# Half-merged weight words and the row norm's root in PSUM, and a second bank for the MLP's second products

## The chip, the cores and the metric

The kernel runs on one core of a Trainium2 chip. The metric is the device time of one execution in microseconds. The chip's engines appear under the names of the profile: PE (TensorE, matrix products), PEld (its weight loads), DVE (VectorE), ACT (ScalarE), POOL (GpSimd) and SP, which issues DMA transfers. SBUF is the on-chip memory, PSUM the banks that PE writes its products into; DVE and ACT read and write both.

## The reference

Three layers follow each other; their inputs are fp32, the first one's shape is (2 samples, 8 heads, 768 tokens, 64).

```python
# 1 attention within buckets
q_bits = (einsum('bhsd,dk->bhsk', q, proj) > 0);  k_bits likewise       # 6 bits
mask = q_bucket[:, :, :, None] == k_bucket[:, :, None, :]
scores = where(mask, q @ k.T / 8, -1e9)
x = softmax(scores) @ v                      # -> (2, 768, 512)
# 2 Fourier mixing and an MLP
u = x + real(fft(fft(x, axis=1), axis=2))
un = (u - mean(u)) / sqrt(var(u) + 1e-6)
x = u + maximum(un @ w_ch1, 0) @ w_ch2       # 512 -> 2048 -> 512
# 3 gated MLP
h = gelu(x @ w_in);  u, v = halves of h      # 512 -> 1024
v_s = w_sg @ (layernorm(v) * g_ln) + b_sg    # over the 768 tokens
out = x + (u * v_s) @ w_out
```

The weights arrive as 64-bit floats, and the kernel makes 32-bit ones of them on the chip.

## The kernel before

Each product that needs fp32 accuracy is made of three f16 products: both factors are split into a high part and a residue (`hl`, `h`, the two halves of a weight region), and `HH` lists the three pairs. So a matrix that is used must be loaded, brought to 32 bits, scaled by a power of two and split.

*Weights.* `weight` (L197 to L239) does this for every matrix. It loads a matrix in pieces into a buffer `wide` (L215). For each piece three DVE steps shift and combine the two 32-bit halves of every word: L219 and L220 work on the high half and leave a half-merged word `t`, L221 adds the low half. Result and half-merged word lie in the same place, the matrix's region. The second MLP matrix, `w2`, has 8 regions of 1024 columns in two pieces each, so 16 pieces of 512; there are two `wide` buffers for it. `w_in` (16 pieces of 256), `w_out` (8) and `w_sg` come later, also with two buffers. After the last piece of a matrix the sum of its squares goes through one PE instruction (`pb`, L136), which gives the scale.

*Sample 0 and sample 1.* Attention works through the heads of sample 0 and then of sample 1. Per group of 128 queries there are a reduction on DVE (`nm`, L397), the exponential on ACT (L399), and a split of it on POOL (`eh`, L251; 128x768 elements). The FFT of a sample ends in tiles of 128 rows `xu` (L590, L591), whose mean and variance are collected (L599, L600). `norm` (L607) then makes 1/sqrt of the variance (`rsqrt`, L108: a first guess by integer steps and three rounds of L115 to L117), scales the rows by a power of two (`un`, L631), splits them (ACT L632, POOL L633) and has them transposed by a DMA into `unT`. For sample 0 all six tiles share one root (6 elements a row), for sample 1 each pair of tiles has its own.

*The MLP.* `ch` (L639) takes 256 rows at a time, a chunk; there are three chunks for a sample. A chunk has 16 groups c1 of 12 matmuls (L657, into a bank of `self.pp`), each followed by a relu on ACT (L663) and its residue on DVE (`h`, L664); sample 1 has 17 buffers for `h`. Then come the second products c2, for each half of the chunk 48 matmuls (L674) into one bank, the only one of the pool `pc`; L678 multiplies it by the row's factor, adds the tile of `xu` and so empties the bank.

*Order.* Three streams are merged by weights: `second` (the rest of attention, then sample 1's FFT), `main0` (sample 0's FFT and MLP) and `prep2` (`w2`). Later the MLP of sample 1 is merged with `side`, which brings the weights of the third layer. A scheduler that follows modelled times then fixes the order of the instructions of each engine from data and buffers; on the chip each engine takes its own queue strictly in that order. `pc` is opened after sample 0's attention; c1 uses the two banks of `pp` and `pp2` in turn until attention is over, and six banks after that. Attention's output has a bank of its own in the pool `pa` (tag `pav`), free once attention is done.

Of the kernel before, what the change touches and what calls it, by code (L numbers as in the profile page):

```python
# [9 lines left out]
F32 = mybir.dt.float32  # L10
FR = mybir.dt.float32r
F16 = mybir.dt.float16
I32 = mybir.dt.int32
AF = mybir.ActivationFunctionType
ALU = mybir.AluOpType
# [5 lines left out]
P = 128  # L21
# [25 lines left out]
LN1 = (True, False)  # L47
# [54 lines left out]
class Kern:  # L102
    def __init__(self, tc, I, out):
        self.tc, self.nc, self.I, self.out = tc, tc.nc, I, out
        self.W = {}


    def rsqrt(self, pool, x, n):  # L108
        nc = self.nc
        y = pool.tile([P, n], F32, tag="rs_y", name="rs_y", bufs=2)  # L110
        t = pool.tile([P, n], F32, tag="rs_t", name="rs_t", bufs=2)
        nc.vector.tensor_scalar(out=y.bitcast(I32), in0=x.bitcast(I32), scalar1=1, scalar2=None, op0=ALU.logical_shift_right)
        nc.vector.tensor_scalar(out=y.bitcast(I32), in0=y.bitcast(I32), scalar1=-1.0, scalar2=float(0x5F3759DF), op0=ALU.mult, op1=ALU.add)
        for _ in range(3):
            nc.vector.tensor_tensor(out=t, in0=y, in1=y, op=ALU.mult)  # L115
            nc.vector.scalar_tensor_tensor(out=t, in0=t, scalar=-0.5, in1=x, op0=ALU.mult, op1=ALU.mult)
            nc.vector.scalar_tensor_tensor(out=y, in0=t, scalar=1.5, in1=y, op0=ALU.add, op1=ALU.mult)  # L117
        return y

# [77 lines left out]
    def weight(self, pool, nm, src, regions, spare, c, q):  # L197

        nc = self.nc
        wide = src.dtype == mybir.dt.int64  # L200
        src = src.bitcast(I32) if wide else src
        sub = WSUB.get(nm, 4)
        m = c // sub
        n = len(regions)
        s, i = self.sc[nm]
        acc = pool.tile([P, 8], F32, tag="wacc", name="wacc", bufs=1)
        tot = pool.tile([P, 1], F32, tag="wm", name="wm", bufs=1)
        for j in range(n):
            if not wide:
                q.dma_start(out=regions[j], in_=src[:, j * c:(j + 1) * c])  # L210
                yield 0.3
            for hf in range(sub if wide else 0):
                o = j * c + hf * m
                x = self.stp.tile([P, 2 * m], I32, tag="wide", name="wide", bufs=self.wb)
                q.dma_start(out=x, in_=src[:, 2 * o:2 * (o + m)])  # L215
                xv = x.rearrange("p (n w) -> p n w", w=2)
                lo, hi = xv[:, :, 0], xv[:, :, 1]
                t = regions[j][:, hf * m:(hf + 1) * m].bitcast(I32)
                nc.vector.tensor_scalar(out=t, in0=hi, scalar1=3, scalar2=0x3FFFFFFF, op0=ALU.logical_shift_left, op1=ALU.bitwise_and)  # L219
                nc.vector.scalar_tensor_tensor(out=t, in0=hi, scalar=-0x40000000, in1=t, op0=ALU.bitwise_and, op1=ALU.bitwise_or)  # L220
                nc.vector.scalar_tensor_tensor(out=t, in0=lo, scalar=29, in1=t, op0=ALU.logical_shift_right, op1=ALU.bitwise_or)  # L221
                yield 0.0029 * m
            nc.scalar.activation(spare[:, 0:c], regions[j], AF.Square, accum_out=acc[:, j:j + 1])
            yield 0.0005 * c
        nc.vector.tensor_reduce(tot, acc[:, 0:n], axis=AX.X, op=ALU.add)
        self.norm_pow2(tot, 2.0 ** 54, s, i, self.pc if nm == "w2" else None)
        yield 1.0
        views = []
        dst = spare
        for j in range(n):  # L230
            d = dst[:, 0:c].bitcast(F16).rearrange("p (t c) -> p t c", t=2)
            nc.scalar.activation(d[:, 0, :], regions[j], AF.Copy, scale=i)
            yield 0.0005 * c
            nc.vector.scalar_tensor_tensor(out=d[:, 1, :], in0=regions[j], scalar=i, in1=d[:, 0, :], op0=ALU.mult, op1=ALU.subtract)
            views.append(d)
            dst = regions[j]
            yield 0.0005 * c
        self.W[nm] = views
        self.spare = dst  # L239
# [367 lines left out]
    def norm(self, fp, up, b, unT, mv, ts):  # L607
        nc, XU = self.nc, self.XU[b]
        t0, w = ts[0], 2 * len(ts)
        x, e, i, s = (fp.tile([P, w], F32, tag=f"ln{j}", name=f"ln{j}", bufs=1 if LN1[b] else 2) for j in range(4))  # L610
        nc.vector.tensor_scalar(out=x.rearrange("p (a c) -> p a c", c=2), in0=mv[:, t0:ts[-1] + 1, :, 1], scalar1=EPS, scalar2=None, op0=ALU.add)
        nc.vector.tensor_scalar(
            out=e.bitcast(I32), in0=x.bitcast(I32), scalar1=24, scalar2=23, op0=ALU.logical_shift_right, op1=ALU.logical_shift_left
# [1 line left out]
        nc.vector.tensor_scalar(  # L615
            out=i.bitcast(I32), in0=e.bitcast(I32), scalar1=-1.0, scalar2=float(190 << 23), op0=ALU.mult, op1=ALU.add
        )
        rs = self.rsqrt(fp, x, w)
        nc.vector.reciprocal(s, i)
        nc.vector.tensor_tensor(out=self.tok[b][:, 2 * t0:2 * t0 + w], in0=rs, in1=s, op=ALU.mult)  # L620
        yield 0.9
# [17 lines left out]
    def ch(self, hp, b, unT, step, tags=None):  # L639
# [27 lines left out]
        def c2(n, j, f):  # L667
            w2 = self.W["w2"]
            if f == 0:
                self.c2t = self.pc.tile([P, 512], F32, tag="c2", name="c2")  # L670
            ps = self.c2t
            wv = w2[f // 2].rearrange("p t (k c) -> p t k c", k=2)[:, :, f % 2, :]
            for m, (a, w) in enumerate(HH):
# [141 lines left out]
    def build(self):  # L815
# [3 lines left out]
        with ExitStack() as ctx:  # L819
# [47 lines left out]

            def second():
                yield from att
                c_att.close()  # L870
                c_s2.close()
                pp3 = c_ps.enter_context(tc.tile_pool(name="pp3", bufs=4, space=PSUM))
# [113 lines left out]
```

## Time and profile before

| | |
|---|---|
| time, median of 3 runs (lowest to highest) | 722.25 us (721.98 to 722.77) |
| the profiled execution: its time, its span | 724.48 us, 722.7 us |
| mean granted clock of TensorE, share of full speed | 0.943 |
| busy time of PE, DVE, ACT, POOL | 645.0, 503.9, 329.8, 273.7 us |
| matmuls: c1 (L657) / c2 (L674) | 1152 in 136.8 us / 576 in 131.8 us |
| three steps of the unpacking of `w2`, 16 pieces | L219 9.0, L220 16.8, L221 17.7 us |

The span is the time from the first to the last instruction of the profiled execution. An engine's busy time says how long it worked, not whether anything waited for it; stretches of some 20 us, the chain of waits that ended last, and single instructions of the timeline show that. An instruction's duration in the timeline includes time in which it has begun and is held up inside, so the same instruction can have two durations. Which part belongs to which time: sample 0's attention ends at about 182 us, the unpacking of `w2` goes from there to 283 us, the rest of attention and sample 1's FFT go on to about 430 us, the MLP of sample 1 ends at 578 us, and the third layer takes the rest.

### The profile page before, as it was taken

The numbers are of one execution on the slowest core, as the hardware profiler recorded it, in microseconds if no ns is written. First come the engines' busy times: TensorE is split into PE (matmuls) and PEld (weight loads), VectorE is DVE, ScalarE is ACT, GpSimd is POOL, SyncE is SP. The second block draws the span as 40 slices with busy tenths as digits, with TensorE's granted clock in tenths as the row PEclk, the third lists the DMA queues.
The fourth block names the chain that finished last, engine by engine and source line by source line (L and its number), as shares of the span: only waits on it lengthen the run. The fifth ranks groups of instructions, "written<-read, shape, count | busy, mean of one in ns | idle before, by whom it ended". The sixth has DMA issues, their size and how long they took to land.

```text
span 722.7 us, 12521 instructions
## 1 busy us (share of the span) xinstructions
PE 645.0 (89%) x4828; PEld 421.8 (58%) x4828; DVE 503.9 (70%) x1095; ACT 329.8 (46%) x517; POOL 273.7 (38%) x232
## 2 busy tenths in 40 slices
PE   3788987976876578999999999979999999999997
PEld 0666677764563357658865766736668444444443
DVE  6999598658999997745435694867562266777663
ACT  5766687764664556745632421423642044222110
POOL 2568588879486465536455041000000012111000
PEclk8899999996886879999999999989999999999999
DMA  8969787999798989737563036552000012011334
GB/s 310 312 182 213 140 175 143 204 202 259 158 235 169 212 193 211 140 67 152 101 128 108 2 60 221 125 148 91 1 1 1 1 35 53 15 29 18 86 88 117
DMA packets 182428, 92.24 MB, mean 128 GB/s; under 512 B 166240, under 2 KB 167008, under 8 KB 181344
## 3 DMA queue, kind: packets, MB, share of 16 engines
q1 hardware_dynamic: 181792, 91.30, 55.0%
q8 instruction: 38, 0.62, 0.4%
q10 hardware_dynamic: 576, 0.14, 0.1%
q14 instruction: 22, 0.18, 0.1%
HBM read 39.50 MB, written 3.15 MB: 59 GB/s over the span
## 4 chain that ended last, share of the span: by engine, by line
PE 56%; DVE 21%; DMA 12%; POOL 4%; issue 3%; ACT 2%; SPq 0%; DVEq 0%; POOLq 0%; ACTq 0%
PE c L674 13%; PE c L657 12%; PE gi L739 9%; PE sg L762 6%; PE s L387 4%; PE go L779 4%; DMA wide<-w_in 3%; DMA et<-eh 3%; DMA wide<-w 3%; DVE nm L397 2%; DVE w L221 2%; DVE w L220 2%; POOL eh L251 2%; DVE k L258 1%; PE y L542 1%
## 5 line engine op out<-in xcount | busy, mean ns | idle before, releaser
L251 POOL TENSOR_TENSOR eh<-e,eh 128x768 f16<-128x768 f32 x80 | 143.4, 1796 | 53.7 <-ACT eh L244 51.0
L657 PE MATMUL c<-unT,w 128*128 128x256 f16 x1152 | 136.8, 277 | 4.2 <-DVE h L664 4.2
L674 PE MATMUL c<-w,h 128*128 128x512 f16 x576 | 131.8, 384 | 5.3 <-DVE xu L678 5.3
L657 PEld LDWEIGHTS <-w 128*128 128x128 f16 x1152 | 113.0, 99 | 22.6 <-issue 5.3
L387 PE MATMUL s<-k,q 128*128 128x384 f32 x384 | 108.1, 413 | 17.8 <-ACT k L282 7.4
L399 ACT ACTIVATE e<-s,nm 128x768 f32<-128x768 f32 x96 | 85.3, 896 | 55.3 <-DVE nm L397 44.7
L397 DVE TENSOR_REDUCE nm<-s 128x1 f32<-128x768 f32 x96 | 90.3, 948 | 22.6 <-PE s L387 21.5
L674 PEld LDWEIGHTS <-h 128*128 128x128 f16 x576 | 56.2, 99 | 69.6 <-issue 9.2
L755 POOL TENSOR_TENSOR vh<-gv,vh 128x512 f16<-128x512 f32 x12 | 13.9, 1156 | 214.0 <-ACT vh L754 214.0
L387 PEld LDWEIGHTS s<-k,q 128*128 128x128 f32 x384 | 72.0, 211 | 30.1 <-ACT k L282 8.3
L455 PE MATMUL pav<-V,et 128*128 128x65 f16 x480 | 56.4, 199 | 19.2 <-DMA et<-eh 13.8
L664 DVE SCALAR_TENSOR_TENSOR h<-c,h 128x256 f16<-128x256 f32 x96 | 39.8, 419 | 36.3 <-ACT h L663 35.8
L246 POOL TENSOR_SCALAR eh<-e 128x768 f16<-128x768 f32 x48 | 47.9, 999 | 36.8 <-ACT e L399 30.7
L455 PEld LDWEIGHTS <-et 128*128 128x128 f16 x480 | 46.0, 102 | 26.1 <-DMA et<-eh 17.7
L456 PE MATMUL pav<-V,et 128*128 128x64 f16 x480 | 56.2, 197 | 0.0
L457 PE MATMUL pav<-V,et 128*128 128x65 f16 x480 | 56.2, 199 | 0.0
L456 PEld LDWEIGHTS <-et 128*128 128x128 f16 x480 | 46.5, 101 | 7.7 <-issue 6.9
L739 PE MATMUL gi<-in,xT 128*128 128x512 f16 x216 | 50.5, 379 | 0.0
L663 ACT ACTIVATE h<-c 128x256 f16<-128x256 f32 x96 | 34.6, 377 | 34.6 <-PE c L657 34.2
L739 PEld LDWEIGHTS <-xT 128*128 128x128 f16 x288 | 28.2, 98 | 35.0 <-issue 1.1
L457 PEld LDWEIGHTS <-et 128*128 128x128 f16 x480 | 46.5, 101 | 1.5 <-issue 0.8
L762 PE MATMUL sg<-vh,sg 128*128 128x512 f16 x180 | 40.8, 379 | 0.0
(198 smaller groups left out, 1009.9 us busy)
## 6 DMA issues: line engine op xcount, KB each, us to landing
wide<-w SPq DMA_DIRECT2D x8, 1024.0 KB, 8.9
wide<-w SPq DMA_DIRECT2D x16, 512.0 KB, 4.3
x<-qk SPq DMA_DIRECT2D x16, 384.0 KB, 4.5
k<-q SPq DMA_DIRECT2D x26, 192.0 KB, 4.1
wide<-w_in SPq DMA_DIRECT2D x16, 256.0 KB, 3.5
vst<-v SPq DMA_DIRECT2D x8, 396.0 KB, 5.3
y<-ot SPq DMA_DIRECT2D x12, 256.0 KB, 2.3
q<-q SPq DMA_DIRECT2D x13, 192.0 KB, 3.9
```

The lines of the kernel that those rows point to most:

```text
L246: self.nc.gpsimd.tensor_scalar(out=out, in0=src, scalar1=scale, scalar2=1.0, op0=ALU.mult, op1=ALU.mult)
L251: (self.nc.vector if eng == "D" else self.nc.gpsimd).tensor_tensor(out=out, in0=a, in1=b, op=ALU.subtract)
L387: nc.tensor.matmul(s[:, hf, 0:HS], q[:, qs], k[:, hf * HS:(hf + 1) * HS], start=n == 0, stop=n == len(pairs) - 1)
L397: nc.vector.tensor_reduce(nm, x["s"], axis=AX.XY, op=ALU.max, negate=True)
L399: nc.scalar.activation(e.rearrange("p (a c) -> p a c", a=2), x["s"], AF.Exp, bias=nm)
L455: nc.tensor.matmul(pv[:, qt, 0:65], et[:, kb, :], V[:, hl, kb, 64:129], start=kb == 0, stop=False)
L456: nc.tensor.matmul(pv[:, qt, 0:64], et[:, kb, :], V[:, hl, kb, 0:64], start=False, stop=False)
L457: nc.tensor.matmul(pv[:, qt, 0:65], et[:, NT + kb, :], V[:, hl, kb, 64:129], start=False, stop=kb == NT - 1)
L657: nc.tensor.matmul(ps[:, 0:step], w[:, a, fo], uT[:, 4 * u + kc, o * P:o * P + step], start=m == 0, stop=m == 11)
L674: nc.tensor.matmul(ps, hs[n, f][:, a, j * P:(j + 1) * P], wv[:, w, :], start=f + m == 0, stop=f == NF - 1 and m == 2)
L739: nc.tensor.matmul(ps, xT[:, 4 * a + kc, :], w_in[kc][:, w, half * DM:(half + 1) * DM], start=n == 0, stop=n == 11)
L762: nc.tensor.matmul(ps, w_sg[kt][:, w, t * P:(t + 1) * P], vh[b][:, kt, a, :], start=n == 0, stop=n == 17)
```

## The change

The half-merged word of `w2` gets a tile `wt` of its own in the PSUM bank of `pc`: L219 and L220 write there, L221 reads it and writes the region. In `norm` two of the root's tensors, the variance x and the temporary t, lie in one tile `lnp` in a bank of `self.pp`; in every round the root first multiplies x*y and then that by -0.5*y, in place of y*y and -0.5*x, also for the third layer, whose t stays in SBUF. Once attention is over, odd c2 tiles take the bank of `pa` and even ones that of `pc`.

```diff
--- before.py
+++ after.py
@@ -103,17 +103,18 @@
     def __init__(self, tc, I, out):
         self.tc, self.nc, self.I, self.out = tc, tc.nc, I, out
         self.W = {}
-
-
-    def rsqrt(self, pool, x, n):
+        self.c2n, self.att_over = 0, False
+
+
+    def rsqrt(self, pool, x, n, t=None):
         nc = self.nc
         y = pool.tile([P, n], F32, tag="rs_y", name="rs_y", bufs=2)
-        t = pool.tile([P, n], F32, tag="rs_t", name="rs_t", bufs=2)
+        t = pool.tile([P, n], F32, tag="rs_t", name="rs_t", bufs=2) if t is None else t
         nc.vector.tensor_scalar(out=y.bitcast(I32), in0=x.bitcast(I32), scalar1=1, scalar2=None, op0=ALU.logical_shift_right)
         nc.vector.tensor_scalar(out=y.bitcast(I32), in0=y.bitcast(I32), scalar1=-1.0, scalar2=float(0x5F3759DF), op0=ALU.mult, op1=ALU.add)
         for _ in range(3):
-            nc.vector.tensor_tensor(out=t, in0=y, in1=y, op=ALU.mult)
-            nc.vector.scalar_tensor_tensor(out=t, in0=t, scalar=-0.5, in1=x, op0=ALU.mult, op1=ALU.mult)
+            nc.vector.tensor_tensor(out=t, in0=x, in1=y, op=ALU.mult)
+            nc.vector.scalar_tensor_tensor(out=t, in0=t, scalar=-0.5, in1=y, op0=ALU.mult, op1=ALU.mult)
             nc.vector.scalar_tensor_tensor(out=y, in0=t, scalar=1.5, in1=y, op0=ALU.add, op1=ALU.mult)
         return y
 
@@ -215,10 +216,11 @@
                 q.dma_start(out=x, in_=src[:, 2 * o:2 * (o + m)])
                 xv = x.rearrange("p (n w) -> p n w", w=2)
                 lo, hi = xv[:, :, 0], xv[:, :, 1]
-                t = regions[j][:, hf * m:(hf + 1) * m].bitcast(I32)
+                to = regions[j][:, hf * m:(hf + 1) * m].bitcast(I32)
+                t = self.pc.tile([P, 512], F32, tag="c2", name="wt")[:, 0:m].bitcast(I32) if nm == "w2" else to
                 nc.vector.tensor_scalar(out=t, in0=hi, scalar1=3, scalar2=0x3FFFFFFF, op0=ALU.logical_shift_left, op1=ALU.bitwise_and)
                 nc.vector.scalar_tensor_tensor(out=t, in0=hi, scalar=-0x40000000, in1=t, op0=ALU.bitwise_and, op1=ALU.bitwise_or)
-                nc.vector.scalar_tensor_tensor(out=t, in0=lo, scalar=29, in1=t, op0=ALU.logical_shift_right, op1=ALU.bitwise_or)
+                nc.vector.scalar_tensor_tensor(out=to, in0=lo, scalar=29, in1=t, op0=ALU.logical_shift_right, op1=ALU.bitwise_or)
                 yield 0.0029 * m
             nc.scalar.activation(spare[:, 0:c], regions[j], AF.Square, accum_out=acc[:, j:j + 1])
             yield 0.0005 * c
@@ -607,7 +609,9 @@
     def norm(self, fp, up, b, unT, mv, ts):
         nc, XU = self.nc, self.XU[b]
         t0, w = ts[0], 2 * len(ts)
-        x, e, i, s = (fp.tile([P, w], F32, tag=f"ln{j}", name=f"ln{j}", bufs=1 if LN1[b] else 2) for j in range(4))
+        e, i, s = (fp.tile([P, w], F32, tag=f"ln{j}", name=f"ln{j}", bufs=1 if LN1[b] else 2) for j in range(3))
+        ps = self.pp.tile([P, 512], F32, tag="p", name="lnp")
+        x, r = (ps[:, 8 * j:8 * j + w] for j in range(2))
         nc.vector.tensor_scalar(out=x.rearrange("p (a c) -> p a c", c=2), in0=mv[:, t0:ts[-1] + 1, :, 1], scalar1=EPS, scalar2=None, op0=ALU.add)
         nc.vector.tensor_scalar(
             out=e.bitcast(I32), in0=x.bitcast(I32), scalar1=24, scalar2=23, op0=ALU.logical_shift_right, op1=ALU.logical_shift_left
@@ -615,7 +619,7 @@
         nc.vector.tensor_scalar(
             out=i.bitcast(I32), in0=e.bitcast(I32), scalar1=-1.0, scalar2=float(190 << 23), op0=ALU.mult, op1=ALU.add
         )
-        rs = self.rsqrt(fp, x, w)
+        rs = self.rsqrt(fp, x, w, r)
         nc.vector.reciprocal(s, i)
         nc.vector.tensor_tensor(out=self.tok[b][:, 2 * t0:2 * t0 + w], in0=rs, in1=s, op=ALU.mult)
         yield 0.9
@@ -667,7 +671,9 @@
         def c2(n, j, f):
             w2 = self.W["w2"]
             if f == 0:
-                self.c2t = self.pc.tile([P, 512], F32, tag="c2", name="c2")
+                self.c2n += 1
+                other = self.att_over and self.c2n % 2
+                self.c2t = (self.pa if other else self.pc).tile([P, 512], F32, tag="pav" if other else "c2", name="c2")
             ps = self.c2t
             wv = w2[f // 2].rearrange("p t (k c) -> p t k c", k=2)[:, :, f % 2, :]
             for m, (a, w) in enumerate(HH):
@@ -867,6 +873,7 @@
 
             def second():
                 yield from att
+                self.att_over = True
                 c_att.close()
                 c_s2.close()
                 pp3 = c_ps.enter_context(tc.tile_pool(name="pp3", bufs=4, space=PSUM))
```

In the changed kernel line numbers of what follows are one to six higher: L219 is L221 there, L631 L635, L664 L668, L674 L680, L678 L684, and L115 to L117 are L116 to L118.

First place, DVE at the root of sample 0's norm, in the stretch in which `w2` is unpacked (`w_3_2155` and `w_2_2154` are regions of `w2`, `ln_2856` is x, `bst` and `mv` mean and variance, `k`, `vmx`, `sv` and `iv` belong to attention). Before:

```order
L600 BN_AGGR mv<-bst 128x2
L220 SCALAR_TENSOR_TENSOR w_3_2155<-wide,w_3_2155 128x512
L148 RECIPROCAL iv_106<-sv_105 128x1
L611 TENSOR_SCALAR ln_2856<-mv 128x6
L221 SCALAR_TENSOR_TENSOR w_3_2155<-wide,w_3_2155 128x512
L612 TENSOR_SCALAR ln_2857<-ln_2856 128x6
L112 TENSOR_SCALAR rs_y<-ln_2856 128x6
L615 TENSOR_SCALAR ln_2858<-ln_2857 128x6
```

Changed:

```order
L223 SCALAR_TENSOR_TENSOR w_2_2154<-wide,wt 128x512
L615 TENSOR_SCALAR lnp<-mv 128x6
L149 RECIPROCAL iv_106<-sv_105 128x1
L221 TENSOR_SCALAR wt<-wide 128x512
L616 TENSOR_SCALAR ln_2866<-lnp 128x6
L113 TENSOR_SCALAR rs_y<-lnp 128x6
L222 SCALAR_TENSOR_TENSOR wt<-wide,wt 128x512
L619 TENSOR_SCALAR ln_2867<-ln_2866 128x6
```

The half-merged word now carries the name `wt`, and only L223 names the region; x is `lnp`. The root's first steps stand between the steps of a piece before and after, but about one piece of `w2` earlier.

Second place, PE in the MLP of sample 1, at the end of the first chunk's first second product (c_5910 before, c_5922 in the changed kernel; h_5906 and h_5918 are its last h). Before:

```order
L674 LDWEIGHTS h_5906
L674 MATMUL c_5910<-w_6_2158,h_5906 128x512
L657 LDWEIGHTS w_0_148
L657 MATMUL c_6053<-unT,w_0_148 128x256
L657 LDWEIGHTS w_0_148
L657 MATMUL c_6053<-unT,w_0_148 128x256
```

Changed:

```order
L680 LDWEIGHTS h_5918
L680 MATMUL c_5922<-w_6_2158,h_5918 128x512
L680 LDWEIGHTS h_5614
L680 MATMUL c_5998<-w_8_156,h_5614 128x512
L680 LDWEIGHTS h_5614
L680 MATMUL c_5998<-w_8_156,h_5614 128x512
```

Before, 28 matmuls of the next chunk's c1 follow (c_6053 and on), in the changed kernel the 48 of the chunk's other second product, c_5998, and only then c1.

Third place, DVE at the same time (`in_5614` is the last region of `w_in`, `out_6149` and `out_6150` are the regions of `w_out`, h_6066 and h_6078 the first h of the next chunk). Before:

```order
L219 TENSOR_SCALAR in_5614<-wide 128x256
L220 SCALAR_TENSOR_TENSOR in_5614<-wide,in_5614 128x256
L678 SCALAR_TENSOR_TENSOR xu_82<-c_5910,tok_133,xu_82 128x512
L221 SCALAR_TENSOR_TENSOR in_5614<-wide,in_5614 128x256
L219 TENSOR_SCALAR in_5614<-wide 128x256
L703 TENSOR_REDUCE rmx<-xu_82 128x1
L220 SCALAR_TENSOR_TENSOR in_5614<-wide,in_5614 128x256
L664 SCALAR_TENSOR_TENSOR h_6066<-c_6053,h_6066 128x256
```

Changed:

```order
L223 SCALAR_TENSOR_TENSOR out_6149<-wide,out_6149 128x256
L728 TENSOR_TENSOR hs<-x_s,s_in 128x1 x2
L222 SCALAR_TENSOR_TENSOR out_6150<-wide,out_6150 128x256
L684 SCALAR_TENSOR_TENSOR xu_82<-c_5998,tok_133,xu_82 128x512
L236 SCALAR_TENSOR_TENSOR gsp<-in_5623,i_in,gsp 128x1024
L223 SCALAR_TENSOR_TENSOR out_6150<-wide,out_6150 128x256
L221 TENSOR_SCALAR out_6150<-wide 128x256
L668 SCALAR_TENSOR_TENSOR h_6078<-c_6065,h_6078 128x256
L222 SCALAR_TENSOR_TENSOR out_6150<-wide,out_6150 128x256
```

Before, that first h comes right behind L220 of the last piece of `w_in`; in the changed kernel behind the first step of the sixth piece of `w_out`.

## Rows read from the trace of the kernel before

**Rows 1.** The page's first part: busy us (share of the span) xinstructions.

```profile
PE 645.0 (89%) x4828; PEld 421.8 (58%) x4828; DVE 503.9 (70%) x1095; ACT 329.8 (46%) x517; POOL 273.7 (38%) x232
```

**Rows 2.** Windows: us, then busy of PE, PEld, DVE, ACT, POOL, PEclk, DMA share, GB/s.

```profile
200.00:220.00 20.00, 14.48 (x165) 11.63 (x164) 19.42 (x30) 13.19 (x21) 17.50 (x16) 0.79 0.96 228
240.00:260.00 20.00, 14.21 (x96) 8.96 (x94) 19.93 (x31) 10.75 (x15) 11.88 (x9) 0.77 0.90 198
283.00:300.00 17.00, 16.38 (x164) 11.61 (x162) 13.03 (x24) 13.74 (x23) 12.61 (x10) 1.00 1.09 214
480.00:500.00 20.00, 16.59 (x85) 8.88 (x85) 13.76 (x49) 4.50 (x7) 0.00 (x0) 0.83 0.40 119
```

**Rows 3.** The chain of waits from 180 to 285 us, its shares by line.

```profile
by line: DVE nm L397 12.6%; DMA wide<-w 12.5%; DVE w L221 12.4%; DVE w L220 11.4%; DVE w L219 6.3%; issue 4.9%; DVE un L631 4.7%; PE c L657 4.5%; DVE bst L599 3.4%; PE s L387 3.3%; DVE xu L591 3.3%; DVE k L258 2.5%; DVE rs_t L116 2.4%; PE y
```

**Rows 4.** Groups of DVE, 182 to 283 us: count | busy, mean ns | idle before.

```profile
L221 DVE SCALAR_TENSOR_TENSOR w<-wide,w 128x512 int32<-128x512 int32 x16 | 17.7, 1104 | 0.1
L220 DVE SCALAR_TENSOR_TENSOR w<-wide,w 128x512 int32<-128x512 int32 x16 | 16.8, 1051 | 0.1
L219 DVE TENSOR_SCALAR w<-wide 128x512 int32<-128x512 int32 x16 | 9.0, 560 | 2.7 <-DMA wide<-w 2.7
...
L590 DVE TENSOR_TENSOR xu<-xu,qdu 128x257 f32<-128x257 f32 x3 | 3.0, 994 | 0.0
L116 DVE SCALAR_TENSOR_TENSOR rs_t<-rs_t,ln 128x6 f32<-128x6 f32 x3 | 2.9, 954 | 0.0
...
L117 DVE SCALAR_TENSOR_TENSOR rs_y<-rs_t,rs_y 128x6 f32<-128x6 f32 x3 | 1.4, 480 | 0.0
L587 DVE SCALAR_TENSOR_TENSOR qdu<-p,sx,qdu 128x257 f32<-128x257 f32 x3 | 1.4, 469 | 0.0
```

**Rows 5.** The timeline, 237 to 250 us: start, us, engine, line, tiles [idle before].

```profile
237.90 0.15 DVE L116 SCALAR_TENSOR_TENSOR rs_t<-rs_t,ln 128x6 f32<-128x6 f32 x1
...
242.47 0.68 DVE L220 SCALAR_TENSOR_TENSOR w<-wide,w 128x512 int32<-128x512 int32 x1
...
243.07 0.41 DVE L219 TENSOR_SCALAR w<-wide 128x512 int32<-128x512 int32 x1
...
246.17 1.68 POOL L633 TENSOR_TENSOR hl<-un,hl 128x512 f16<-128x512 f32 x1 [1.08 <-ACT hl L632]
...
246.76 1.64 DVE L220 SCALAR_TENSOR_TENSOR w<-wide,w 128x512 int32<-128x512 int32 x1
...
248.13 1.77 POOL L251 TENSOR_TENSOR eh<-e,eh 128x768 f16<-128x768 f32 x1 [0.28 <-ACT eh L244]
...
248.32 1.60 DVE L116 SCALAR_TENSOR_TENSOR rs_t<-rs_t,ln 128x6 f32<-128x6 f32 x1
```

**Rows 6.** Groups of DVE over the whole run, shapes apart.

```profile
L678 DVE SCALAR_TENSOR_TENSOR xu<-c,tok,xu 128x512 f32<-128x512 f32 x12 | 9.0, 746 | 23.7 <-PE c L674 23.7
...
L765 DVE TENSOR_TENSOR t<-sg,gB 128x512 f32<-128x512 f32 x12 | 8.3, 692 | 15.3 <-PE sg L762 15.3
```

**Rows 7.** The timeline, 446 to 500 us, DVE and PE.

```profile
447.30 0.29 DVE L219 TENSOR_SCALAR in<-wide 128x256 int32<-128x256 int32 x1 [5.01 <-DMA wide<-w_in]
447.50 18.07 PE L657 MATMUL c<-unT,w 128*128 128x256 f16 x164
...
465.40 10.52 PE L674 MATMUL c<-w,h 128*128 128x512 f16 x48
...
468.85 0.29 DVE L219 TENSOR_SCALAR in<-wide 128x256 int32<-128x256 int32 x1 [0.54 <-DMA wide<-w_in]
...
471.59 0.42 DVE L664 SCALAR_TENSOR_TENSOR h<-c,h 128x256 f16<-128x256 f32 x1
...
483.41 8.12 PE L674 MATMUL c<-w,h 128*128 128x512 f16 x26 [4.43 <-DVE xu L678]
...
498.56 0.29 DVE L219 TENSOR_SCALAR out<-wide 128x256 int32<-128x256 int32 x1
```

**Rows 8.** The timeline of PE, 540 to 585 us.

```profile
567.47 10.52 PE L674 MATMUL c<-w,h 128*128 128x512 f16 x48 [0.84 <-DVE xu L678]
```

## The prediction

> **What bounds the kernel now.** I read the busy time of each engine, then the stretches, then the chain of waits, then groups and single instructions where the chain changes engine. The engine row names TensorE (PE): 645.0 of 722.7 us [rows 1]. It is an average over two kinds of stretch. Between about 182 and 283 us, where the second MLP matrix is unpacked beside the first sample's FFT and the second sample's attention, VectorE (DVE) is busy 19.42 and 19.93 us of 20, PE only 14.48 and 14.21, at a granted clock of 0.79 and 0.77 [rows 2]. The chain of that stretch says the same: DVE lines lead it, and L219 to L221, the three steps that turn 64-bit words of the matrix into 32-bit ones, hold 6.3 + 11.4 + 12.4 = 30.1% of its 105 us [rows 3]. From 283 us on PE is full (16.38 of 17 at a clock of 1.00 [rows 2]) but for two places: it stands 4.43 us at 479 us and 0.84 us at 566.6 us, both times for L678 [rows 7, 8].
>
> Why does DVE take so long there? The steps come in two durations: L220 and L221 take 0.68 us, or much more; L219 0.41, or more. In the one shown, L220 starts at 246.76 while GpSimd (POOL) has been at L633 since 246.17; POOL ends at 247.85, L220 at 248.40. The next, L116 on 6 elements a row, starts at 248.32 and takes 1.60 us; POOL's L251 ran 248.13 to 249.90 [rows 5]. A DVE instruction with two SBUF tensors, or the fast one-input L219, thus waits out a POOL instruction. L587, which reads one tensor from PSUM and one from SBUF, took a mean of 469 ns in the same stretch, L590, of the same width but with both in SBUF, 994 [rows 4]. So one SBUF operand is not held up, two are.
>
> **The change, part by part.** *The half-merged word in PSUM.* 16 pieces, three DVE instructions each, now 17.7 + 16.8 + 9.0 = 43.5 us [rows 4]; their floor is 16 x (0.41 + 0.68 + 0.68) = 28.3 us [rows 5]. With the word in PSUM no step has two SBUF inputs, so the 15.2 us above the floor should go, but each step then pays for PSUM. No row shows an integer step that writes PSUM. Bounds: from below the floor, 15.2 us saved; from above 0.746 us for each step, L678's price for 512 elements with one PSUM input, 16 x 2.24 = 35.8, so 7.7 saved [rows 6]. I take L765's 0.692, the nearest row (512 elements, one PSUM and one SBUF input): 16 x 2.08 = 33.2, so 10.3 us saved. L219 alone becomes dearer, 0.41 to 0.69, and that is inside this sum. [...]
>
> *The row norm's root in PSUM.* In the first sample's norm three L116 cost 2.9 us and three L117 1.4 where one not held up takes 0.15 [rows 4, 5]. With x and t in PSUM both keep one SBUF input: 6 x 0.15 = 0.9, saving 3.4 us. The bound on the other side is PSUM's extra, 0.07 by L678 against L220 [rows 5, 6], 0.4 us lost in six steps, if these waits only move to the next instruction with two SBUF tensors. The new first product x*y in place of y*y reads a second tensor, a PSUM one, and costs nothing new there. In the last stage, where t stays in SBUF, x*y reads two SBUF tensors of one element a row, and no wait of PE there names them; so nothing. The norm also borrows one of the two banks that the first product c1 uses until L117's third round. The changed order of DVE has some 22 instructions between sample 0's second scaled tile (L631 before) and that round; c1 waits for its transposes meanwhile, so I take nothing, with up to 5 us if PE stands there.
>
> *How much of 13.7 us is on the path.* The chain carries 30.1% of 105 = 31.6 us of the 43.5 of the unpacking [rows 3], so 31.6/43.5 x 10.3 = 7.5 us of that saving, and 2.4% of L116, 2.5 us, of which 2.1 go. That is 9.6. What is late next: the loads of the matrix, 12.5% of the chain [rows 3], with a DMA share already at 0.96 and 0.90 [rows 2], and the other two-SBUF instructions, L590 among them [rows 4], which inherit some of the waiting. Against that POOL, held up less, hands attention its tiles sooner. I take 9 us; ends 3 and 13. PE is full from 283 us on, so all of it arrives at the end unless something later takes it back.
>
> *Two banks for the second products.* After attention the c2 products alternate between the old bank and attention's. At 479 us PE waited because L678, the instruction that empties the only bank, stood in DVE's queue behind L219 instructions that wait for w_in pieces. That wait, 4.43 us, goes. [...] Together 6.8. At 566.6 us 0.84 goes too [rows 8].
>
> But the order moves with it. Before, two c1 groups of the next chunk ran ahead of that wait, and their h instructions stood on DVE's queue in front of the w_out pieces. Now both second products run back to back and c1 comes after, and DVE meets the first h of that chunk only behind seven w_in and six w_out pieces. PE side, from the end of the c1 of sample 1's first chunk (465.57: 447.50 + 18.07): 96 x 0.219 = 21.0 us of second products, then six c1 groups of 12 x 0.110 (18.07 / 164) = 1.32 us into the six free banks, 28.9 us in all [rows 7]. DVE side: before, the last h of the chunk ended at 472.0, 6.4 us after that point, and the 12 pieces from there to L219 at 498.56 came 26.6 / 12 = 2.2 us apart [rows 7]. So 6.4 + 13 x 2.2 = 35.0, and 0.4 for the h itself: PE stands 6.5 us, and comes out slow for 2.4 as before. 8.9 us for 6.8: 2.1 us lost. Bounds: no standing if the pieces come at 1.7 us (6.8 won); at the 3.1 us of the eight pieces before, which stood between h instructions (447.30 to 468.85, seven steps [rows 7]), 18.2 us and 2.4, so 13.8 lost. I take 2.1 lost: no h stands between the pieces now, so the later pace is the nearer.
>
> **Sum.** 9.0 - 2.1 + 0.8 = 7.7 us off the span of 722.7, so 715.0; the profiled execution took 724.5, 1.8 around the span, so 716.8 for such a run. The runs' median is 722.25, 0.3% under the profiled one; the same 7.7 us off it gives 714.6, and I say 714.5.
>
> **The rivals.** *Both gains hold.* The w_in and w_out pieces come sooner, since DVE's root instructions no longer hold up the FFT in front of them, or at 1.7 us each: 9.0 + 6.8 + 0.8 = 16.6, 705.7. For it: a wide piece needs no PE. Against: every piece is three DVE steps and a load, and 2.2 us is what they took with the least beside them. 20%.
>
> *The loads bound the stretch instead.* A DMA share of 0.96 and 0.90 leaves little if the queues can't go over 1: 101 us at their mean of 0.93 is 94 us of transfers; with the transposes waiting for their turn only 3 us come off. 3.0 - 2.1 + 0.8 = 1.7, 720.6. Against it: the share is 1.09 from 283 us on [rows 2], and only 2.7 us of L219's idle time is put down to loads [rows 4]. 13%.
>
> *Slower: the tail is paced by the pieces, not by PE.* Place: DVE's queue between the last h of sample 1's first chunk and the first h of the next. If a piece takes 3.1 us instead of 2.2, because the transposes of the other sample's rows stand between them on the load queue, PE stands 6.4 + 13 x 3.1 + 0.4 - 28.9 = 18.2 us, with 2.4 slow, 20.6 in place of 6.8: 13.8 lost against 9.8 won, 726.2. It turns the sign from 2.8 us a piece on (14.3 us of standing and 2.4, for 6.8 with 9.8 won). For it: the eight pieces before came at that pace. Against: those waited for PE between. 9%.
>
> *The change doesn't do what it says:* a PSUM write by an integer step is held up all the same, so L219 to L221 stay at 43.5 us, and the tail's 2.1 lost and 0.8 won are left: 723.5, in the band of no change. 4%.
>
> **How the numbers follow.** The forecast, a stretch shorter by 6 to 12 us and a tail that gains or loses 4, has 54%; its own range is 708.5 to 719. The range for 8 in 10 goes from 703.5, to take in most of the first rival, to 722, past the loads' case. About 0.2% is what a measurement can tell from no change, 720.8 to 723.7. Faster than that: 54 + 20 and eight of the loads' 13, 0.82; the other five and the 4 of the last case, 0.09, no change; slower 0.09.
>
> **What would show it.** In the changed profile L219's line should show near 0.69 us with little spread, and the two below it near 0.70, none above 0.9; the 6-element root steps near 0.16 to 0.25. The second matrix should be done near 274 us instead of 283, with PE full from there. At about 470 us there should be no wait of a second product for L678; instead PE should stand before c1 of the next chunk, or at the norm matmul of w_in, for DVE. At the last second product no 0.84. Wrong would be: steps of 0.9 us or more in PSUM (the price), DVE idle in front of L219 for more than 6 us in all (the loads), PE waiting at sample 0's first c1 for the root (the borrowed bank), or a tail without a wait (the piece count).

## The result, and the profile after

The changed kernel takes 714.02 us (median of 4 runs, 711.1 to 716.46); the kernel before, timed beside it, 722.12 us. The ratio on record is 0.9861, with a 95% interval of 0.9821 to 0.9902, so it is faster by 1.4%; the two medians by themselves give 0.9888 (8.1 us), which lies inside that interval. Timed again on another occasion (e5 below) the ratio was 0.9867. The forecast was 714.5 us.

The page's first part of the changed kernel: PE is 5 us less busy and the span 9.1 us shorter (713.6).

```profile
PE 639.9 (90%) x4828; PEld 414.1 (58%) x4828; DVE 494.2 (69%) x1095; ACT 330.1 (46%) x517; POOL 266.5 (37%) x232
```

The stretches that answer to [rows 2], columns as there. DVE is still full between 200 and 220 us, and PE is busy for less of that stretch than before (12.62 us against 14.48, at a clock of 0.87 against 0.79); the gain shows from 260 to 283 us, where DVE is no longer full and PE is busy for 21.23 of 23 us, at a clock of 1.00.

```profile
200.00:220.00 20.00, 12.62 (x129) 9.35 (x128) 20.00 (x38) 13.35 (x21) 16.71 (x17) 0.87 0.98 214
...
260.00:283.00 23.00, 21.23 (x257) 17.92 (x256) 17.45 (x38) 16.18 (x28) 12.13 (x11) 1.00 1.10 240
...
480.00:500.00 20.00, 19.49 (x150) 15.06 (x151) 15.98 (x46) 7.80 (x13) 0.00 (x0) 0.91 0.27 88
```

The kernel before from 260 to 283 us, for comparison:

```profile
260.00:283.00 23.00, 16.59 (x164) 13.61 (x165) 20.47 (x28) 11.81 (x21) 10.94 (x9) 0.85 0.97 207
```

The whole stretch of the unpacking, 182 to 283 us, in one row each: first the kernel before, PE 73.44 us at a mean clock of 0.82,

```profile
182.00:283.00 101.00, 73.44 (x650) 51.79 (x649) 94.54 (x149) 55.69 (x84) 60.29 (x47) 0.82 0.89 195
```

then the changed kernel, PE 81.16 us at 0.89. The DMA share rises from 0.89 to 0.99.

```profile
182.00:283.00 101.00, 81.16 (x787) 56.85 (x786) 89.73 (x168) 65.40 (x101) 62.63 (x54) 0.89 0.99 214
```

The groups of DVE in it, which answer to [rows 4] (count | busy, mean ns of one | idle before). The three steps of the unpacking, L221 to L223 here, take 0.675 to 0.688 us each and 32.8 us in all, where they took 43.5. The root's steps L117 and L118 are down to 0.16 us. But L635 (the scaled rows), L624 and L619, which still have all their tensors in SBUF, are long.

```profile
L222 DVE SCALAR_TENSOR_TENSOR wt<-wide,wt 128x512 int32<-128x512 int32 x16 | 11.0, 688 | 0.1
L221 DVE TENSOR_SCALAR wt<-wide 128x512 int32<-128x512 int32 x16 | 11.0, 688 | 2.5 <-DMA wide<-w 2.4
L223 DVE SCALAR_TENSOR_TENSOR w<-wide,wt 128x512 int32<-128x512 int32 x16 | 10.8, 675 | 0.0
L635 DVE TENSOR_SCALAR un<-xu,mv,ln 128x512 f32<-128x512 f32 x6 | 7.4, 1226 | 0.0
...
L624 DVE TENSOR_TENSOR tok<-rs_y,ln 128x6 f32<-128x6 f32 x1 | 1.5, 1542 | 0.0
...
L619 DVE TENSOR_SCALAR ln<-ln 128x6 int32<-128x6 int32 x1 | 1.1, 1085 | 0.0
...
L118 DVE SCALAR_TENSOR_TENSOR rs_y<-lnp,rs_y 128x6 f32<-128x6 f32 x3 | 0.5, 166 | 0.0
...
L117 DVE SCALAR_TENSOR_TENSOR lnp<-lnp,rs_y 128x6 f32<-128x6 f32 x3 | 0.5, 160 | 0.0
```

Two rows from the timeline show a step that is no longer held up: L221 starts while POOL is at work on L253, and is done long before it.

```profile
239.28 1.83 POOL L253 TENSOR_TENSOR eh<-e,eh 128x768 f16<-128x768 f32 x1
...
239.52 0.73 DVE L221 TENSOR_SCALAR wt<-wide 128x512 int32<-128x512 int32 x1
```

The same holds for all the steps. In the kernel before, 15 of the 32 L220 and L221 start while a POOL instruction is under way. For 13 of these it has more than 0.06 us to go: they take 0.92 to 2.91 us, and each ends 0.54 to 0.55 us after the end of that POOL instruction or of one right behind it. The other 19 take 0.64 to 0.69 us. In the changed kernel 28 of the 48 steps start while a POOL instruction is under way, and none takes more than 0.74 us.

The last piece of `w2` is done at 274.9 us, and in the kernel before at 281.2 (not at 283, where the windows end and where the prediction's sign has it), so 6.3 us earlier. In the MLP of sample 1 the timeline of PE, which answers to [rows 7, 8], shows no wait of a second product any more. PE stands 4.45 us in another place, before the norm matmul `pb` of `w_in`, goes through the next 11 matmuls at 0.384 us each (0.219 is their pace elsewhere; the granted clock is 0.59 from 480.35 to 484.5 and 1.00 from 458 to 475), and after seven groups of c1 waits 0.38 us for the chunk's second h (493.64 on DVE).

```profile
436.22 21.12 PE L661 MATMUL c<-unT,w 128*128 128x256 f16 x192
457.18 18.51 PE L680 MATMUL c<-w,h 128*128 128x512 f16 x85
480.14 0.35 PE L137 MATMUL pb<-wm,ones 128*128 128x1 f32 x2 [4.45 <-issue]
480.35 4.22 PE L680 MATMUL c<-w,h 128*128 128x512 f16 x11
...
494.12 12.11 PE L661 MATMUL c<-unT,w 128*128 128x256 f16 x108 [0.38 <-DVE h L668]
...
569.74 0.81 PE L745 MATMUL gi<-gsp,xT 128*128 128x512 f16 x3 [0.84 <-DVE xu L684]
```

DVE beside it. After the last h of the chunk (463.13) come the pieces; `pb` waits for `wm` (L227, 479.88), the sum over the squares of the last region of `w_in`, whose last piece starts at 475.74. The sixth piece of `w_out` starts at 491.24, and the next chunk's first h right behind it.

```profile
463.13 0.41 DVE L668 SCALAR_TENSOR_TENSOR h<-c,h 128x256 f16<-128x256 f32 x1
...
475.74 0.28 DVE L221 TENSOR_SCALAR in<-wide 128x256 int32<-128x256 int32 x1
...
479.88 0.16 DVE L227 TENSOR_REDUCE wm<-wacc 128x1 f32<-128x4 f32 x1 [0.35 <-ACT gsp L225]
...
491.24 0.29 DVE L221 TENSOR_SCALAR out<-wide 128x256 int32<-128x256 int32 x1
491.45 0.42 DVE L668 SCALAR_TENSOR_TENSOR h<-c,h 128x256 f16<-128x256 f32 x1
```

Two marks split the gain. The first second product of sample 1 starts at 457.18 instead of 465.40 us: 8.2 us came before it. The first product of the third layer starts at 569.74 instead of 578.84, so 0.9 us came between the marks, and nothing after them (143.8 us remain in both). These 9.1 us are of one execution of each kernel.

### The profile page after: what moved, and what is told of

Its sections match the earlier page's. It is cut to its first block, busy times and chain, and to the rows that moved or that the text cites. A ratio compares the mean times of both kernels' runs of the same rounds, so it can differ in the third digit from the quotient of the medians.

```text
span 713.6 us, 12540 instructions
## 1 busy us (share of the span) xinstructions
PE 639.9 (90%) x4828; PEld 414.1 (58%) x4828; DVE 494.2 (69%) x1095; ACT 330.1 (46%) x517; POOL 266.5 (37%) x232
## 4 chain that ended last, share of the span: by engine, by line
PE 45%; DVE 8%; DMA 7%; ACT 2%; POOL 1%; issue 1%; SPq 1%; DVEq 0%; ACTq 0%
PE c L661 11%; PE c L680 10%; PE gi L745 9%; PE sg L768 7%; PE go L785 4%; DMA wide<-w_in 3%; PE s L389 2%; DMA wide<-w_out 2%; DVE w L236 1%; DMA et<-eh 1%; PE p L570 1%; PE y L544 1%; DMA k<-q 1%; DMA xT<-ghl 1%; ACT w L234 1%
## 5 line engine op out<-in xcount | busy, mean ns | idle before, releaser
L253 POOL TENSOR_TENSOR eh<-e,eh 128x768 f16<-128x768 f32 x80 | 140.7, 1762 | 57.1 <-ACT eh L246 54.3
L680 PE MATMUL c<-w,h 128*128 128x512 f16 x576 | 130.7, 382 | 1.0 <-DVE w L236 1.0
L389 PE MATMUL s<-k,q 128*128 128x384 f32 x384 | 107.1, 405 | 15.1 <-ACT k L284 10.7
L680 PEld LDWEIGHTS <-h 128*128 128x128 f16 x576 | 56.1, 99 | 65.6 <-issue 3.8
L389 PEld LDWEIGHTS s<-k,q 128*128 128x128 f32 x384 | 70.2, 208 | 26.3 <-ACT k L284 10.8
L457 PE MATMUL pav<-V,et 128*128 128x65 f16 x480 | 53.8, 195 | 20.5 <-DMA et<-eh 20.0
L457 PEld LDWEIGHTS <-et 128*128 128x128 f16 x480 | 44.3, 99 | 34.6 <-DMA et<-eh 27.4
L668 DVE SCALAR_TENSOR_TENSOR h<-c,h 128x256 f16<-128x256 f32 x96 | 39.4, 418 | 31.0 <-ACT h L667 30.4
L248 POOL TENSOR_SCALAR eh<-e 128x768 f16<-128x768 f32 x48 | 46.1, 961 | 37.0 <-ACT e L401 27.1
L458 PE MATMUL pav<-V,et 128*128 128x64 f16 x480 | 53.6, 193 | 0.0
L459 PE MATMUL pav<-V,et 128*128 128x65 f16 x480 | 53.4, 195 | 0.0
L458 PEld LDWEIGHTS <-et 128*128 128x128 f16 x480 | 44.8, 98 | 2.2 <-issue 1.4
L459 PEld LDWEIGHTS <-et 128*128 128x128 f16 x480 | 44.8, 98 | 0.8 <-issue 0.2
```

The lines of the kernel that those rows point to most:

```text
L248: self.nc.gpsimd.tensor_scalar(out=out, in0=src, scalar1=scale, scalar2=1.0, op0=ALU.mult, op1=ALU.mult)
L253: (self.nc.vector if eng == "D" else self.nc.gpsimd).tensor_tensor(out=out, in0=a, in1=b, op=ALU.subtract)
L389: nc.tensor.matmul(s[:, hf, 0:HS], q[:, qs], k[:, hf * HS:(hf + 1) * HS], start=n == 0, stop=n == len(pairs) - 1)
L457: nc.tensor.matmul(pv[:, qt, 0:65], et[:, kb, :], V[:, hl, kb, 64:129], start=kb == 0, stop=False)
L458: nc.tensor.matmul(pv[:, qt, 0:64], et[:, kb, :], V[:, hl, kb, 0:64], start=False, stop=False)
L459: nc.tensor.matmul(pv[:, qt, 0:65], et[:, NT + kb, :], V[:, hl, kb, 64:129], start=False, stop=kb == NT - 1)
```

## The experiments

Times are medians; the ratio is to the kernel before in the same runs, its 95% interval in brackets, and what a change gains in us is worked out from it. Rows of a profile are of one execution. Each kernel has its own line numbers: without the root's edits they are two lower from the norm on than in the changed kernel (L633 for L635 in e1), and e9 has those of before up to L436.

**e1, the half-merged word alone.** From the changed kernel, the root and the second products are put back:

```diff
-        ps = self.pp.tile([P, 512], F32, tag="p", name="lnp")
-        x, r = (ps[:, 8 * j:8 * j + w] for j in range(2))
+        x, e, i, s = (fp.tile(...) for j in range(4))  # and y*y, -0.5*x in rsqrt
-                other = self.att_over and self.c2n % 2
+                other = False
```

> Only the half-merged word of w2 lies in PSUM; root and second products are as before. Theory A (the steps of the unpacking are no longer held up by POOL, and 9 us of the stretch come off, most of it from them): 5 to 7.5 us faster, 0.990 to 0.993 of before; the three steps near 0.69, 0.69 and 0.68 us. Rival B (the root was the expensive part, since its waits stand in front of the FFT): under 3 us faster, above 0.996. Rival C (the second bank makes the gain): no change.

Measured: 714.12 us, ratio 0.9878 (0.9847 to 0.9908), 8.8 us faster: more than A's figure, and B and C fall. The steps are as long as in the whole change (0.684, 0.684 and 0.676 us). The word alone thus gives all of the whole change's gain that these times can show (714.12 against 714.02 us). The groups of its root, 182 to 283 us, for comparison with e4:

```profile
L633 DVE TENSOR_SCALAR un<-xu,mv,ln 128x512 f32<-128x512 f32 x6 | 4.9, 823 | 0.0
...
L117 DVE SCALAR_TENSOR_TENSOR rs_t<-rs_t,ln 128x6 f32<-128x6 f32 x3 | 2.8, 948 | 0.0
...
L614 DVE TENSOR_SCALAR ln<-ln 128x6 int32<-128x6 int32 x1 | 1.8, 1755 | 0.0
L118 DVE SCALAR_TENSOR_TENSOR rs_y<-rs_t,rs_y 128x6 f32<-128x6 f32 x3 | 1.7, 568 | 0.0
L116 DVE TENSOR_TENSOR rs_t<-rs_y 128x6 f32<-128x6 f32 x3 | 1.5, 516 | 0.0
...
L622 DVE TENSOR_TENSOR tok<-rs_y,ln 128x6 f32<-128x6 f32 x1 | 0.6, 598 | 0.0
```

**e2, the root alone.**

```diff
-                t = self.pc.tile([P, 512], F32, tag="c2", name="wt")[...] if nm == "w2" else to
+                t = to
-                other = self.att_over and self.c2n % 2
+                other = False
```

> Only the row norm's root lies in PSUM, with x*y first; the unpacking and the second products are as before. A: 1 to 3 us faster, 0.996 to 0.999; the root's steps of sample 0 near 0.16 us. B: over 5 us faster, below 0.993. C: no change. If the waits only move to the next instruction with two SBUF tensors, no change and the same sum for that group and its neighbours.

Measured: 720.7 us, ratio 0.9974 (0.9953 to 0.9995): 1.9 us faster, as A has it. The steps L117 and L118 came to 1.0 us in place of 4.3. The three steps of the unpacking, still in SBUF, stay long; their sum is 42.5 us.

```profile
L223 DVE SCALAR_TENSOR_TENSOR w<-wide,w 128x512 int32<-128x512 int32 x16 | 19.1, 1192 | 0.1
L222 DVE SCALAR_TENSOR_TENSOR w<-wide,w 128x512 int32<-128x512 int32 x16 | 13.6, 851 | 0.1
L221 DVE TENSOR_SCALAR w<-wide 128x512 int32<-128x512 int32 x16 | 9.8, 612 | 3.2 <-DMA wide<-w 3.2
...
L117 DVE SCALAR_TENSOR_TENSOR lnp<-lnp,rs_y 128x6 f32<-128x6 f32 x3 | 0.5, 161 | 0.0
...
L118 DVE SCALAR_TENSOR_TENSOR rs_y<-lnp,rs_y 128x6 f32<-128x6 f32 x3 | 0.5, 154 | 0.0
```

**e3, the second bank alone.**

```diff
-                t = self.pc.tile([P, 512], F32, tag="c2", name="wt")[...] if nm == "w2" else to
+                t = to                                # and the root back in SBUF, as in e1
```

> Only the second bank for the second products. A: it gives a wait of some 4.4 us back as another one and comes out between 1 us faster and 2 us slower, 0.998 to 1.003. C: it makes the gain, 5 us or more faster, below 0.993. In both the 4.43 us wait of a second product for L678 is gone.

Measured: 725.95 us, ratio 1.0038 (1.0014 to 1.0062): 2.7 us slower, a little more than A's bound, and C falls. The wait of 4.43 us is gone, but others are there: 2.29 us for an h in c1 of the first chunk, 1.71 for `pb`, 1.10 and 1.05 for h in the next chunk. The first chunk's 192 c1 matmuls need 25.1 us (445.25 to 470.35) where they need 21.1 elsewhere.

```profile
445.25 11.97 PE L659 MATMUL c<-unT,w 128*128 128x256 f16 x108
459.51 11.00 PE L659 MATMUL c<-unT,w 128*128 128x256 f16 x84 [2.29 <-DVE h L666]
470.35 15.05 PE L678 MATMUL c<-w,h 128*128 128x512 f16 x69
487.11 0.35 PE L137 MATMUL pb<-wm,ones 128*128 128x1 f32 x2 [1.71 <-issue]
...
502.27 1.47 PE L659 MATMUL c<-unT,w 128*128 128x256 f16 x12 [1.10 <-DVE h L666]
504.80 11.95 PE L659 MATMUL c<-unT,w 128*128 128x256 f16 x108 [1.05 <-DVE h L666]
```

**e4, word and root, one bank.**

```diff
-                other = self.att_over and self.c2n % 2
+                other = False
```

> Word and root in PSUM, second products in one bank as before. A: 7 to 9 us faster, 0.987 to 0.990, as the whole change within 1 us, with the wait of 4 to 5 us for L684 in the MLP of sample 1 back. C: 2 us faster at most.

Measured: 714.4 us, ratio 0.9878 (0.9837 to 0.9918). The wait for L684 is back, 4.32 us. The whole change stands at 0.9861 and 0.9867, so the second bank is worth some 1 us with the word in PSUM, less than these intervals tell apart. And the root adds nothing to the word alone that the times show (0.9878 both). The groups say where a part of its saving went. L116, L117 and L118 take 0.5 us each here and 1.5, 2.8 and 1.7 in e1, 4.5 less in all, and L616, which now reads PSUM, takes 0.1 instead of 1.8 (L614 in e1). But L635 takes 7.3 instead of 4.9 (L633 in e1), L624 1.5 instead of 0.6 (L622 in e1), and L619 1.0 instead of 0.2 (L617 in e1). Over all of sample 0's norm, 16 steps on 6 elements a row and six scaled tiles, 12.2 us stand against 14.2 in e1, so 2.0 us of DVE time are left of the saving:

```profile
L635 DVE TENSOR_SCALAR un<-xu,mv,ln 128x512 f32<-128x512 f32 x6 | 7.3, 1223 | 0.0
...
L624 DVE TENSOR_TENSOR tok<-rs_y,ln 128x6 f32<-128x6 f32 x1 | 1.5, 1547 | 0.0
...
L117 DVE SCALAR_TENSOR_TENSOR lnp<-lnp,rs_y 128x6 f32<-128x6 f32 x3 | 0.5, 160 | 0.0
```

**e5, the whole change again**, timed beside the next three.

> The whole change, timed beside the next three. Both theories: 0.985 to 0.989 of before.

Measured: 713.92 us, ratio 0.9867 (0.9834 to 0.9900).

**e6, four buffers for the pieces of the third layer's weights.**

```diff
-            self.stp, self.wb = c_r.enter_context(tc.tile_pool(name="stp", bufs=1, side=R)), 2
+            self.stp, self.wb = c_r.enter_context(tc.tile_pool(name="stp", bufs=1, side=R)), 4
```

> The whole change, and four instead of two buffers for the loaded pieces of w_in, w_out and w_sg. Theory D (a piece takes 2 us there because with two buffers its load of 2.8 us can't start before the piece two ahead is done; that pace makes the wait of 4.45 us at the norm matmul of w_in): the wait goes with the slow stretch behind it, 5 to 6.5 us off the whole change, 0.977 to 0.981 of before. Rival E (the pace is the DMA queue's or DVE's own): no change against the whole change, 0.985 to 0.989.

Measured: 709.05 us, ratio 0.9791 (0.9755 to 0.9828); by the ratio 5.5 us off the whole change, by the medians 4.9: D holds, E falls. This beats both kernels. `pb` no longer waits: DVE is at the last piece of `w_in` at 462.18 and at `wm` at 467.47 (475.74 and 479.88 in the changed kernel), and PE comes to `pb` at 470.01 only. Between the two marks it takes 107.8 us (455.77 to 563.61) in place of 112.6. That is less than the 6.3 us of the wait and the slow matmuls behind it, since two waits for h in the next chunk, 0.99 and 1.03 us, are new. PE in the timeline, then DVE:

```profile
455.77 14.41 PE L680 MATMUL c<-w,h 128*128 128x512 f16 x66
470.01 0.28 PE L137 MATMUL pb<-wm,ones 128*128 128x1 f32 x2
...
563.61 0.81 PE L745 MATMUL gi<-gsp,xT 128*128 128x512 f16 x3 [0.84 <-DVE xu L684]
```

```profile
462.18 0.29 DVE L221 TENSOR_SCALAR in<-wide 128x256 int32<-128x256 int32 x1
...
467.47 0.15 DVE L227 TENSOR_REDUCE wm<-wacc 128x1 f32<-128x4 f32 x1
```

**e7, four buffers, word and root, one bank** (e6 and the edit of e4).

> Word and root in PSUM, second products in one bank, four buffers for the pieces. D: the wait for L684 at the second product goes as well, since DVE no longer stands in front of it, and the time is that of the two-bank kernel with four buffers within 2 us: then the second bank is worth 0.84 us at most. Rival F (the second bank is what is needed): within 2 us of word and root alone, near 0.988.

Measured: 711.18 us, ratio 0.9836 (0.9799 to 0.9873), 2.1 us above e6 by the medians and 3.3 by the ratios, with intervals that overlap; below e4 by about as much (3.0 by the ratios). So it lies between D and F, and neither holds as it stands: D had the wait for L684 gone, and 2.60 us of it are left. What the second bank is worth beside four buffers stays open:

```profile
469.86 12.18 PE L680 MATMUL c<-w,h 128*128 128x512 f16 x48 [2.60 <-DVE xu L684]
```

**e8, four buffers, the root in SBUF** (e6 with the root put back).

> The word of w2 in PSUM, second bank and four buffers; the root in SBUF as before. If the root's held-up steps only hand their wait on (as word and root against the word alone suggest): the same as the whole change with four buffers within 1.5 us. If the root saves its own 3 us: 2 to 3 us slower than that.

Measured: 709.74 us, ratio 0.9798 (0.9765 to 0.9830): 0.7 us from e6. With the word in PSUM the root's bank makes no difference that these runs can tell, the second such pair after e1 and e4; but each pair is uncertain by some 3 us, so a saving of 2 us is not excluded either.

**e9, POOL made small.** From the kernel before:

```diff
-            self.sub(c[i % len(c)], x["eh"][:, 1, :], x["e"], x["eh"][:, 0, :])
+            ...                                        # sample 0 as it was; sample 1:
+                self.nc.scalar.activation(x["eh"][:, 1, 0:704], x["e"][:, 0:704], AF.Copy)
+                self.sub("P", x["eh"][:, 1, 704:768], x["e"][:, 704:768], x["eh"][:, 0, 704:768])
```

> The kernel before, but for sample 1 POOL's subtraction covers 64 of 768 columns, and ACT writes a copy into the other 704 in place of the residue (so attention's low parts of sample 1 are not the reference's). A (the unpacking's steps are held up by POOL): L219 near 0.41 to 0.45 us, L220 and L221 near 0.70 to 0.80 on the mean, without PSUM, the sum of 43.5 us at 30 to 34. Rival G (the long durations come from DVE's own queue or from loads into SBUF): the means stay near 0.56, 1.05 and 1.10. The time of the whole is not to be compared, as ACT has more to do.

Measured: without any PSUM the three steps fall to 0.521, 0.797 and 0.792 us in 182 to 283 us; 16 pieces at these means are 33.8 us (43.5 before, 32.8 in the changed kernel). The rows hold 14 pieces: the first two come before 182 us here, where POOL's work is as before, and with them the sum is 36.1. A holds and G falls; L219 is higher than A's figure: of the ten from 200 to 257 us one took 1.80 us and nine 0.39 to 0.52, and POOL is not silent (six L637 of 1.24 us are left, and others). DVE first, then POOL, whose main instruction is 0.43 us long in place of 1.78:

```profile
L220 DVE SCALAR_TENSOR_TENSOR w<-wide,w 128x512 int32<-128x512 int32 x14 | 11.2, 797 | 0.1
L221 DVE SCALAR_TENSOR_TENSOR w<-wide,w 128x512 int32<-128x512 int32 x14 | 11.1, 792 | 0.1
L219 DVE TENSOR_SCALAR w<-wide 128x512 int32<-128x512 int32 x14 | 7.3, 521 | 7.7 <-DMA wide<-w 7.6
```

```profile
L251 POOL TENSOR_TENSOR eh<-e,eh 128x64 f16<-128x64 f32 x24 | 10.3, 429 | 28.1 <-ACT eh L244 26.6 <-DMA et<-eh 1.0
```

**e10, the word of the first MLP matrix in PSUM too.** From e6:

```diff
-WSUB = {'w1': 1, 'w2': 2}
+WSUB = {'w1': 2, 'w2': 2}                              # and six wide buffers of half the size
-                t = self.pc.tile([P, 512], F32, tag="c2", name="wt")[...] if nm == "w2" else to
+                t = (self.pc.tile(...) if nm == "w2" else self.pp.tile(...))[...] if nm in ("w1", "w2") else to
```

> The whole change with four buffers, and the half-merged word of w1 in PSUM too: 16 pieces of 512 in place of 8 of 1024 (six wide buffers of half the size), the word in the one bank of pp. Theory A with the price measured: its three steps cost 6.1 + 14.6 + 12.2 = 32.9 us in SBUF, and 16 x 3 x 0.685 = 32.9 us in PSUM, so nothing is gained: 0.976 to 0.983 of before, as four buffers alone; the steps near 0.69, 0.69, 0.68. Rival H (a word in PSUM is worth it wherever a matrix is unpacked, as it frees POOL too): 4 us more off, 0.974 or less. Rival I (the bank of pp is also used by attention, and PE waits for it): slower than four buffers alone, above 0.985.

Measured: 713.48 us, ratio 0.9858 (0.9819 to 0.9897), 4.4 us above e6's median, with intervals that just overlap: no gain, so H falls. The price of the steps is as A says (0.680 to 0.688), but the time is I's. That the shared bank is the cause is read from the waits, and more on DVE than on PE: L221 stood 4.1 us until ACT had read `oT` out of that bank, while PE's waits for L223 there come to 1.2 us. A bank of its own for this word was not tried.

```profile
L221 DVE TENSOR_SCALAR wt<-wide 128x512 int32<-128x512 int32 x32 | 22.0, 688 | 10.6 <-DMA wide<-w 6.5 <-ACT oT L454 4.1
...
L223 DVE SCALAR_TENSOR_TENSOR w<-wide,wt 128x512 int32<-128x512 int32 x32 | 21.7, 680 | 0.3
```

## Why the prediction was right

**The mechanism.** It said that a DVE step with two SBUF tensors, or the fast one-input step, waits out a POOL instruction, and that one SBUF operand is not held up. The changed kernel shows it by a group that no longer varies (0.675 to 0.688 us), the single steps by where they end (0.54 to 0.55 us after a POOL instruction), and e9 by the other side: less POOL, short steps, no PSUM. "One SBUF operand is not held up" holds for the steps here whose other operand or output lies in PSUM (0.74 us at most). L635 and L619, which read one SBUF tensor and write another, are held up as L219 is: in the changed kernel four of the six L635 take 1.07 to 1.97 us and end 0.28 to 0.29 us after a POOL instruction, and L619 takes 1.09 and ends 0.03 after one; the six L219 of before that take 0.58 to 1.08 us end 0.28 after one.

**The step's price.** Taken: 0.692 us from L765, so 33.2 us for 48 steps. Measured: 0.688, 0.688 and 0.675, 32.8 us, a saving of 10.7 where 10.3 was put. Even the one-input step, 0.41 us in SBUF when not held up [rows 5], takes 0.688 once it writes PSUM.

**The part on the path.** Put at 7.5 us for the word, by its share of the chain. The word alone gave 8.8 us (6.7 to 11.1 by the interval), which agrees. The loads did not become the bound: DVE stood only 2.5 us before L221, and the DMA share went up to 0.99 over the stretch and to 1.10 from 260 to 283 us, which was the weak point of the rival of the loads.

**The root.** The prediction added 2.1 us for it to those of the word. This is the term of the sum that the runs bear out least. The root's steps shrank as said (L117 and L118: 1.0 us in place of 4.3), and alone it gives 1.9 us (0.4 to 3.4 by the interval). Beside the word it gives 0.0 us (e4 against e1) and 0.7 (e6 against e8), each uncertain by some 3 us, so the times alone do not tell 2.1 us from nothing. The traces show that a part of the wait is handed on to steps that still have their tensors in SBUF. Sample 0's whole norm takes 14.2 us of DVE in e1 and 14.4 in e8, and with the root in PSUM 12.2 in e4 and 11.3 in e6. So 2 to 3 us of DVE time are saved, of which the kernel's time shows 0.7 at most; where the rest goes stays open. The prediction named the handing on as a bound, "if these waits only move to the next instruction with two SBUF tensors", and chose the other end. The bank that the norm borrows cost nothing that the profile shows: no wait of PE in the changed kernel names the root.

**How near the sum came.** Up to the first mark 8.2 us came off where 9 was forecast, behind it 0.9 were won where 1.3 were to be lost. The word gave 1.3 us more than its term and the root 1.4 to 2.1 less, both within the intervals. That 714.02 us lies half a microsecond from the 714.5 forecast is therefore in part luck: the 7.7 us forecast stand against 8.1 between the medians, 9.1 between the two profiled executions and 10 by the ratio.

**The tail.** Put at 2.1 us lost and 0.84 won; measured 0.9 won in all. The DVE side was right in its number: thirteen pieces from the last h (463.54, its end) to 491.24 are 2.13 us apart, 2.2 forecast, and the first h of the next chunk comes at 491.45. So was the exchange of one wait for another. Wrong was where PE stands: the sum had 6.5 us before c1 and did not count that `pb` for `w_in` lies among the second products and needs the same pieces, though the signs to look for named that place. The 2.4 us for slow matmuls, which the sum has both in its 6.8 and in its 8.9, is what the 26 matmuls behind the wait of 4.43 us took in the kernel before beyond the pace elsewhere: 0.312 us each in place of 0.219, at a granted clock of 0.71 (483.41 to 491.53 us; 1.00 from 465.4 to 475.9). In the changed kernel PE stood at `pb` for 4.45 us, was slow for (0.384 - 0.219) x 11 = 1.8, and so came to c1 late enough to wait 0.38 only. So 6.6 us came in place of the 8.9 of the sum, for the 6.8 that went away; and of two waits of 0.84 us for L678 one went.

**The rivals.** "Both gains hold" needed quicker pieces. e6 makes them so by buffers, and is 4.9 us faster than the whole change (709.05 against 713.92): what this rival had in view was there to be had, but not by this change. The slower rival did not come about in the whole change; e3 is a case of its kind, one chunk earlier: with the second bank alone PE waits for an h of the first chunk, and the kernel is 2.7 us slower. Why the scheduler's order is that much worse without the word's change is read from the order and the waits alone; it was not tried apart.

## What to carry to other kernels

When one instruction has two durations, look at what the other engine does while the long one runs; a group's mean hides it, and a single row of the timeline beside the other engine's shows it. An intermediate value that moves to PSUM stopped being held up here, at a price of some 0.68 us for each step of 512 elements. So it pays where the hold-ups cost more than that price (43.5 against 32.8 us for `w2`) and not where they cost the same (32.9 against 32.9 for `w1`, and there in a bank that attention needs too), and the saving on a second such group may in part only pass the wait to the steps that are left. A bank added in front of an engine moved instructions here: count who now stands behind whom, and ask for the pace of what paces them, here two load buffers.

## What was not expected

An instruction on 6 elements a row can be held up as long as a wide one, and also with a single SBUF tensor to read: in e1 L614 took 1.755 us, where the same step from PSUM (L616) takes 0.147 in e4, and in the changed kernel L619 took 1.085, up to 0.03 us after the end of a POOL instruction, where the same step (L617 in e1) takes 0.158. Both read and write SBUF, as L219 does. The prediction had this for two SBUF tensors and for the wide L219 only, so it did not see L635 and L619 among those that would take over the root's waits.
